# A path that is not taken: its transfers move from SyncE to GpSimd, and ScalarE issues the store of its last output tile

## The chip, the cores and the metric

One core of one Trainium2 chip runs the kernel. The metric is device time in microseconds: three runs of the kernel gave 161.3, 161.39 and 161.57, median 161.39. A further execution was taken with the hardware profiler; its own time was 161.53.

## The reference

Four batches with eight heads of 768 tokens and 64 channels each. An 8 x 8 matrix per head, made doubly stochastic in five rounds, mixes the eight blocks of 96 keys and values; attention runs inside each block; a gated MLP follows, whose gate mixes tokens with a 768 x 768 matrix.

```
for _ in range(5):
    P = exp(P - max(P)); P /= sum(P, rows) + 1e-9; P /= sum(P, columns) + 1e-9
k_sorted, v_sorted = P @ blocks of k, P @ blocks of v
attn = softmax(scale * q_b @ k_sorted.T) @ v_sorted          # inside blocks of 96
h = relu(x @ w_in); u, v = halves of h                       # x: heads side by side
v_n = (v - mean(v)) / sqrt(var(v) + 1e-6)
out = (u * (w_spatial @ v_n + b_spatial)) @ w_out
```

## The kernel before

The kernel has two versions of the whole computation. The *main path* is quick and leaves out the subtraction of maxima. It is written out by hand: the string `ORDER` (lines 18 to 51) lists some 300 short units by name and arguments, and the loop at line 769 records them one after the other. Every engine works through its own instructions in that order and waits on semaphores for the others. The *general path* (`general_path`, line 724) computes the same with maxima subtracted, in plain loops over batches and head pairs, using the same units.

Which of them gives the output is decided on the chip. Unit `CK` (line 694) compares row sums, column sums and reciprocals of the main path with bounds, `CF` (line 709) counts the violations into a flag, and `LF` (line 715) loads that flag into a register of each of the five engines. At line 773 each engine tests its register: with a flag above zero it runs the general path, otherwise it jumps over it. With the inputs drawn here the flag is zero and no instruction of the general path is executed. Unit `BH` (line 718) gives PE and VectorE a hint of the jump.

```
with tc.If(st["beyond"] > 0, preferred_fallthrough_block=True, label="general"):
    general_path()
```

For an If, the framework builds a second block, the *else block*, for the engines that jump. [...] So each engine that does something in the general path has in the else block, for each semaphore it would have raised, an instruction that waits until its main-path work is counted and then adds what the general path would have added. Transfers issued by SyncE or ScalarE count on eight semaphores in turn (the hardware transfers), those issued by GpSimd on eight others; for the latter one instruction of GpSimd, INC_SWDGE_SEM, adds to all eight. Then comes the *end block* (line 800 in the profile): SyncE waits for every semaphore once more in twelve steps, and after its drain all engines meet in a barrier which GpSimd gathers and releases, twice.

The output is stored by rows of 128 tokens. For the last batch (3), the six row blocks go one by one: `OH` multiplies, `OI` evicts PSUM to SBUF on ScalarE (`A`) or VectorE (`D`), `OJ` (line 690) issues the store, all on SyncE's queue. The last units of `ORDER` evict and store in this order:

```
... OI:D:3:0:0:512 OI:D:3:5:256:512 OI:A:3:4:0:512 OJ:3:1:0:512 OJ:3:5:256:512 OJ:3:4:0:512
OJ:3:0:0:512
```

Evictions are at lines 110 (ScalarE) and 112 (VectorE), the last stores at line 692, those of the batches before at line 645. In the general path SyncE loads `sort_net` (line 184), copies the block-shaped values (`VC`, line 418), transposes the attention output by DMA (`XD`, line 501) and stores the output (`OS`, line 645). `XT` (line 506) is a unit that makes the same transposition on TensorE, with a copy out of PSUM; the main path uses both.

Of the kernel before, what the change touches and what calls it, by code (L numbers as in the profile page):

```python
# [45 lines left out]
SH:3:3:0:0 GH:D:3:0:0 SH:0:3:0:1 OS:2:2 SH:1:3:1:1 GH:P:3:1:1 SH:2:3:3:1 OH:3:3:2:0:512:0:4 GH:D:3:0:1 OS:2:0:0:1  # L46
OS:2:0:1:2 OH:1:3:3:0:512:0:4 GH:P:3:3:1 OI:A:3:2:0:512 OI:A:3:3:0:512 OJ:3:2:0:512 OH:2:3:5:0:256:0:4 OJ:3:3:0:512
OH:0:3:5:256:512:0:4 OI:D:3:5:0:256 OH:3:3:1:0:512:0:4 OH:2:3:0:0:512:0:4 OI:A:3:1:0:512 OJ:3:5:0:256
OH:1:3:4:0:512:0:4 OI:D:3:0:0:512 OI:D:3:5:256:512 OI:A:3:4:0:512 OJ:3:1:0:512 OJ:3:5:256:512 OJ:3:4:0:512
OJ:3:0:0:512  # L50
"""

# [13 lines left out]
def kernel(  # L66
# [12 lines left out]
    nc = tc.nc  # L79

    B, H, S, D = q.shape
# [8 lines left out]
    KC = DM // 128  # L90
    FC = DH // 128
    HP = H // 2
# [11 lines left out]

    def ps_tile(n, dt=FP32):
        return psum.tile([128, 2, 512 if dt == FP32 else 1024], dt, name=f"ps{n}", tag=f"ps{n}")

    def copy(eng, out, in_):
        if eng == "A":
            nc.scalar.copy(out=out, in_=in_)  # L110
        else:
            nc.vector.tensor_copy(out=out, in_=in_)
# [9 lines left out]
    p_all = const.tile([BH, NB, NB], FP32, name="p_all")  # L122
# [27 lines left out]
    st = {}  # L150
# [30 lines left out]
            nc.gpsimd.dma_start(out=w_out_sb, in_=moe_w_out.rearrange("(fc p) n -> p fc n", p=128))  # L181

    def load_sort_net():
        nc.sync.dma_start(out=p_all, in_=sort_net.rearrange("b h i j -> (b h) i j"))

    def u_S0():
        load_sort_net()
# [37 lines left out]
    def u_SK(n, safe=False):  # L225
        n = int(n)
        rows, cols = (first[:, 0:NB], first[:, NB:2 * NB]) if n == 0 else (rowsum, colsum)
        over_rows = lambda x: x.to_broadcast([BH, NB, NB])
        over_cols = lambda x: _raw_ap(x, 0, [x.ap[0], [0, NB], x.ap[1]])
        if safe:  # L230
            nc.vector.reduce_max(out=rowsum, in_=p_all, axis=AX.X)
            nc.vector.tensor_sub(out=p_all, in0=p_all, in1=over_rows(rowsum))
        nc.scalar.activation(out=p_all, in_=p_all, func=AF.Exp)
        nc.vector.reduce_sum(out=rows, in_=p_all, axis=AX.X)
        if safe:
            nc.vector.tensor_scalar_add(out=rows, in0=rows, scalar1=1e-9)
        nc.vector.reciprocal(out=rowsum, in_=rows)
        nc.vector.tensor_mul(out=p_all, in0=p_all, in1=over_rows(rowsum))
        nc.vector.reduce_sum(out=cols, in_=p_all.rearrange("p i j -> p j i"), axis=AX.X)
        if safe:  # L240
            nc.vector.tensor_scalar_add(out=cols, in0=cols, scalar1=1e-9)
        nc.vector.reciprocal(out=colsum, in_=cols)
        to = p16.rearrange("p (i j) -> p i j", i=NB) if n == 4 else p_all
        nc.vector.tensor_mul(out=to, in0=p_all, in1=over_cols(colsum))
        if n == 4:
            nc.vector.transpose(out=p_t, in_=p16)

    def u_PR(ps):
        pr = ps_tile(ps)[:, 0, 0:NB * BH].rearrange("p (i y) -> p i y", i=NB)
        for i in range(NB):  # L250
            nc.tensor.matmul(
                pr[:, i, :], lhsT=spread[:, (i % NI) * NB:(i % NI + 1) * NB].rearrange("p j t -> p (j t)"),
                rhs=p_t[:, (i // NI) * BH:(i // NI + 1) * BH], start=True, stop=True,
            )
        st["pr"] = pr
# [6 lines left out]
    def u_P0(lo, hi):  # L262
        lo, hi = int(lo), int(hi)
        n, pr = hi - lo, st["pr"]
        nc.vector.tensor_mul(
            out=pd(0)[:, lo:hi].rearrange("p h (i t) -> p h i t", t=TB),
            in0=_raw_ap(mask16, 0, [mask16.ap[0], [0, n], [0, NB], [1, TB]]),
            in1=_raw_ap(pr, lo, [pr.ap[0], [1, n], [BH, NB], [0, TB]]),
        )

    def u_PC(eng):
        copy(eng, prep_sb, st["pr"])

    def u_PD(b, lo, hi):
        b, lo, hi = int(b), int(lo), int(hi)
        n = hi - lo
        nc.gpsimd.tensor_mul(
            out=pd(b)[:, lo:hi].rearrange("p h (i t) -> p h i t", t=TB),
            in0=_raw_ap(mask16, 0, [mask16.ap[0], [0, n], [0, NB], [1, TB]]),
            in1=_raw_ap(prep_sb, b * H + lo, [prep_sb.ap[0], [1, n], [BH, NB], [0, TB]]),  # L280
        )
# [103 lines left out]
    def u_KT(ps, eng, b, hp):  # L385
        mixed("k", "kT", ps, eng, int(b), int(hp))
# [14 lines left out]
    def u_VM(ps, eng, b, hp):  # L401
        b, hp = int(b), int(hp)
        t = ps_tile(ps)
        for hh in range(2):
            nc.tensor.matmul(
                t[:, hh, 0:G * D], lhsT=pd(b)[:, 2 * hp + hh, :], rhs=st["v", b][:, 2 * hp + hh, :],
                start=True, stop=True,
            )
        copy(
            eng,  # L410
            vm[:, :, 2 * hp:2 * hp + 2, 0:D].rearrange("p g h d -> p h g d"),
            t[:, :, 0:G * D].rearrange("p h (g d) -> p h g d", g=G),
        )

    def u_VC(b, lo, hi):
        b = int(b)
        for i in range(int(lo), int(hi)):
            nc.sync.dma_start(
                out=vb[b % 2][:, i].rearrange("c h d -> c (h d)"),
                in_=vm[i * TB:(i + 1) * TB].rearrange("t g h d -> t g (h d)"),  # L420
            )
# [75 lines left out]
    def u_XD(b, ih, lo=0, hi=4):  # L497
        b, ih, lo, hi = int(b), int(ih), int(lo), int(hi)
        if ("xT", b) not in st:
            st["xT", b] = att.tile([128, 2, KC, HW], BF16, name="xT", tag="xT", bufs=2)  # L500
        nc.sync.dma_start_transpose(
            out=st["xT", b][:, ih, lo:hi].rearrange("p k (i c) -> p (k i) c", i=NI),
            in_=st["x", b, ih][:, lo:hi].rearrange("p k i c -> p (k i c)"),
        )

    def u_XT(ps, eng, b, ih, lo):
        b, ih, lo = int(b), int(ih), int(lo)
        if ("xT", b) not in st:
            st["xT", b] = att.tile([128, 2, KC, HW], BF16, name="xT", tag="xT", bufs=2)
        t = ps_tile(ps, BF16)[:, 0, 0:2 * HW].rearrange("p (k i c) -> p k i c", k=2, i=NI)  # L510
        for k in range(2):
            for i in range(NI):
                nc.tensor.transpose(t[:, k, i, :], st["x", b, ih][:, lo + k, i, :], ident[0:BLK, 0:BLK])
        copy(eng, st["xT", b][:, ih, lo:lo + 2].rearrange("p k (i c) -> p k i c", i=NI), t)
# [54 lines left out]
    def u_LN(b, lo, hi):  # L569
        b, lo, hi = int(b), int(lo), int(hi)  # L570
        mv, rs = st["mv", b], st["rs", b]
        nc.scalar.activation(out=rs[:, lo:hi], in_=mv[:, lo:hi, 1], func=AF.Ln, bias=eps_tile[:], scale=1.0)
        nc.scalar.activation(out=rs[:, lo:hi], in_=rs[:, lo:hi], func=AF.Exp, bias=0.0, scale=-0.5)
# [66 lines left out]
            st["o", b, n0] = ld.tile([128, 3, DM], FP32, name="o_sb", tag="ld")[:, 0:2]  # L640
        copy(eng, st["o", b, n0][:, lo:hi], st["o_ps", b, n0][:, lo:hi])

    def u_OS(b, n0, lo=0, hi=2):
        b, n0, lo, hi = int(b), int(n0), int(lo), int(hi)
        nc.sync.dma_start(
            out=out[b].rearrange("(c p) n -> p c n", p=128)[:, n0 + lo:n0 + hi, :],
            in_=st["o", b, n0][:, lo:hi],
        )
# [38 lines left out]
        st["o1", b, n, c0] = ld.tile([128, 3, DM], FP32, name="o1_sb", tag="ld")[:, 0, 0:c1 - c0]  # L687
        copy(eng, st["o1", b, n, c0], st["o1_ps", b, n, c0])

    def u_OJ(b, n, c0, c1):  # L690
        b, n, c0, c1 = (int(x) for x in (b, n, c0, c1))
        nc.sync.dma_start(out=out[b, n * 128:(n + 1) * 128, c0:c1], in_=st["o1", b, n, c0])

    def u_CK():
        nc.vector.memset(bad, 0.0)
# [28 lines left out]
    def general_path():  # L724


        st.clear()
        load_sort_net()
        for n in range(5):
            u_SK(n, safe=True)  # L730
        u_PR(0)
        u_P0(0, 8)
        u_PC("A")
        for b in range(B):
            if b > 0:
                u_PD(b, 0, 8)
            for x in ("q", "k", "v"):
                u_L(x, b, 0, H)
            for hp in range(HP):
                u_VM(2, "A", b, hp)  # L740
            u_VC(b, 0, NB)
            for hp in range(HP):
                u_QN(2, "A", b, hp)
                u_KT(3, "D", b, hp)
                for ih in range(2):
                    u_SM(b, hp, ih)
                    u_AT(2, b, hp, ih)
            for ih in range(2):
                u_XD(b, ih, 0, HP)
            for n in range(0, G, 2):  # L750
                u_VP(n % 4, "A", b, n, n + 1)
                u_ST(b, n)
                u_ST(b, n + 1)
            u_LN(b, 0, G)
            for n in range(G):
                u_LA(b, n)
            for m in range(2):
                for ih in range(2):
                    u_UP(2 * m + ih, "A", b, m, ih)
            for mc in range(FC):  # L760
                u_SP(mc, b, mc)
                u_GT("D", b, mc)
            for n in range(0, G, 2):
                u_OP(n % 4, b, n)
                u_OE("A", b, n)
                u_OS(b, n)
# [38 lines left out]
```

## Time and profile before

| what | value |
|---|---|
| median of three runs | 161.39 us |
| the profiled execution's own time | 161.53 us |
| its span, first to last instruction | 159.7 us |
| granted TensorE clock, mean over the span | 0.996 |
| busy: PE / VectorE / ScalarE / GpSimd | 147.6 / 113.1 / 85.7 / 42.2 us |
| output stores on SyncE, 256 KB each | 7, median 2.6 us from issue to landing |

Busy time counts arithmetic alone; branches, semaphore steps and the issuing of transfers are not in it, and rows of an engine's sequencer carry a q after its name (SPq, ACTq). PE is busy through nearly all of the span except its very end, the last two of forty slices:

```profile
PE   6997989999999999999999999999999999899840
DMA  3999999999999999950000657300911377037253
```

The span ends with the last step of the barrier, not with the last store or the last piece of arithmetic. The profiled execution's own time is 1.8 us longer than its span.

### The profile page before, as it was taken

To read this page: it belongs to the slowest core of one execution; us is meant where nothing else is said; L and a number is where in the kernel's file an instruction comes from. 1 tells how busy PE (TensorE), PEld (TensorE's weight loads), DVE (VectorE), ACT (ScalarE), POOL (GpSimd) and SP (SyncE) were. 2 spreads that over 40 slices of the span, in tenths; PEclk is the share of its full clock that TensorE was granted. 3 is DMA by queue.
4 is the path that set the end of the run, shared out by engine and by line. 5 is a ranking of instruction groups with operands and counts; after the bars stand their busy time and mean duration, and the time that the engine had idled before them with its cause. 6 is when DMAs were issued, how large, how long until landed. Compare 5 with 4: busy or idle time off the path is not lost. (4 is left out here: it accounts for less than half of the span.)

```text
span 159.7 us, 3977 instructions
## 1 busy us (share of the span) xinstructions
PE 147.6 (92%) x1647; PEld 89.2 (56%) x1661; DVE 113.1 (71%) x261; ACT 85.7 (54%) x117; POOL 42.2 (26%) x46
## 2 busy tenths in 40 slices
PE   6997989999999999999999999999999999899840
PEld 2355867845686668556465654655655554455410
DVE  4786889638995679867838669897558956947620
ACT  3556799968889409478572446555432242340220
POOL 7942782292000034040000650210004440005300
PEclk9999999999999999999999999999999999999998
DMA  3999999999999999950000657300911377037253
GB/s 84 259 204 204 204 208 202 208 224 239 269 207 202 204 226 241 214 92 4 0 4 0 123 90 131 61 4 0 290 71 34 69 259 266 0 137 259 96 202 112
DMA packets 27526, 23.58 MB, mean 148 GB/s; under 512 B 7280, under 2 KB 24432, under 8 KB 27504
## 3 DMA queue, kind: packets, MB, share of 16 engines
q0 software_dynamic: 14352, 11.80, 46.6%
q1 hardware_dynamic: 13152, 11.49, 25.1%
q8 instruction: 14, 0.23, 0.6%
q14 instruction: 8, 0.07, 0.2%
HBM read 24.78 MB, written 6.29 MB: 195 GB/s over the span
## 5 line engine op out<-in xcount | busy, mean ns | idle before, releaser
L620 POOL TENSOR_TENSOR gt<-z,u_sb 128x768 bf16<-128x768 f32 x10 | 16.4, 1642 | 76.1 <-DVE rec_all L490 55.1
L442 ACT ACTIVATE ex<-ps 96x768 bf16<-96x768 f32 x32 | 24.4, 804 | 7.9 <-PE ps L437 7.8
L604 PE MATMUL ps<-wspT,v_sb 128*128 128x384 bf16 x144 | 25.4, 326 | 0.0
L592 PE MATMUL ps<-xT,w_in_sb 128*128 128x384 bf16 x128 | 23.3, 326 | 0.6 <-ACT o_sb L110 0.6
L491 DVE TENSOR_TENSOR x_sb<-ps,rec_all 96x512 bf16<-96x512 f32 x32 | 22.0, 687 | 1.1
L549 PE MATMUL ps<-w_in_sb,xT 128*128 128x512 bf16 x88 | 21.6, 379 | 0.5 <-issue 0.2
L566 DVE BATCH_NORM_STATS2 stats<-v_sb 128x6 f32<-128x512 bf16 x24 | 16.3, 680 | 5.5 <-ACT v_sb L116 4.3
L610 DVE TENSOR_TENSOR z<-ps,b_bc 128x768 f32<-128x768 f32 x12 | 11.5, 956 | 11.2 <-PE ps L604 11.2
L604 PEld LDWEIGHTS <-v_sb 128*128 128x128 bf16 x144 | 13.3, 98 | 8.4
L116 ACT ACTIVATE u_sb<-ps 128x768 bf16<-128x768 f32 x15 | 12.2, 812 | 10.8 <-PE ps L592 7.9
L116 ACT ACTIVATE v_sb<-ps 128x1024 bf16<-128x1024 f32 (+1 forms) x10 | 9.8, 982 | 14.4 <-PE ps L549 14.4
L592 PEld LDWEIGHTS <-w_in_sb 128*128 128x128 bf16 x128 | 11.8, 98 | 8.7 <-issue 0.9
L630 PE MATMUL ps<-w_out_sb,gt 128*128 128x512 bf16 x68 | 16.3, 379 | 0.2
L110 ACT COPY o_sb<-ps 128x1024 f32<-128x1024 f32 (+1 forms) x10 | 8.4, 839 | 14.7 <-PE ps L680 10.6
L549 PEld LDWEIGHTS <-xT 128*128 128x128 bf16 x96 | 8.9, 98 | 9.8
L483 PEld LDWEIGHTS <-ex 96*128 96x128 bf16 x256 | 10.9, 97 | 3.8 <-DVE x_sb L491 0.3
L483 PE MATMUL ps<-vb,ex 96*128 96x65 bf16 x256 | 12.4, 193 | 0.1
L110 ACT CAST kt<-ps 128x768 bf16<-128x768 f32 x12 | 9.3, 804 | 5.9 <-PE ps L378 5.9
L221 PE MATMUL ps<-warm 128*128 128x512 bf16 x35 | 10.0, 441 | 1.3 <-DVE warm L194 1.3
L630 PEld LDWEIGHTS <-gt 128*128 128x128 bf16 x72 | 6.6, 98 | 7.1
L437 PE MATMUL ps<-qT,kt 64*128 64x96 bf16 x256 | 9.3, 204 | 0.5 <-DVE x_sb L491 0.2
L490 DVE RECIPROCAL rec_all<-ps 96x8 f32<-96x8 f32 x32 | 6.3, 197 | 4.8 <-PE ps L483 4.4
(94 smaller groups left out, 198.5 us busy)
## 6 DMA issues: line engine op xcount, KB each, us to landing
out_dram<-o_sb SPq DMA_DIRECT2D x8, 512.0 KB, 3.7
k_in<-in_k_dram POOLq DMA_DIRECT2D x4, 768.0 KB, 23.9
v_in<-in_v_dram POOLq DMA_DIRECT2D x4, 768.0 KB, 22.8
vb<-vm SPq DMA_DIRECT2D x24, 99.0 KB, 5.6
q_in<-in_q_dram POOLq DMA_DIRECT2D x3, 768.0 KB, 29.0
out_dram<-o_sb SPq DMA_DIRECT2D x7, 256.0 KB, 2.6
ws_in<-in_moe_w_spatial_dram POOLq DMA_DIRECT2D x2, 576.0 KB, 27.8
w_in_sb<-in_moe_w_in_dram POOLq DMA_DIRECT2D x2, 512.0 KB, 23.9
```

The costliest lines, as they stand in the source:

```text
L110: nc.scalar.copy(out=out, in_=in_)
L116: nc.scalar.activation(out=out, in_=in_, func=AF.Relu)
L442: nc.scalar.activation(out=e_tile(b, hp, ih).rearrange("p h (x g) -> p h x g", g=G), in_=t[0:BLK, :, 0:HW].rearrange("p h (g x) -> p h x g ...
L483: nc.tensor.matmul(t[:, hh, ii * VW:ii * VW + D + 1], lhsT=e[:, c:c + 128], rhs=vb[b % 2][:, ih * NI + ii, 2 * hp + hh, 0:D + 1], start=Tr ...
L491: nc.vector.tensor_mul(out=x_sb[:, hp].rearrange("p i (h d) -> p h i d", h=2), in0=tv[:, :, :, 0:D], in1=_raw_ap(rec, 0, [rec.ap[0], [NI, ...
L549: nc.tensor.matmul(t[:, x, :], lhsT=st["xT", b][:, n // 3, kc, (n % 3) * 128:(n % 3 + 1) * 128], rhs=w_in_sb[:, kc, DH:DFF], start=(kc == ...
L566: nc.vector.bn_stats(out=stats, in_=st["v_sb", b, n])
L592: nc.tensor.matmul(t[:, x, 0:HW], lhsT=w_in_sb[:, kc, mc * 128:(mc + 1) * 128], rhs=st["xT", b][:, ih, kc, :], start=(kc == 0), stop=(kc = ...
L604: nc.tensor.matmul(t[:, x, 0:HW], lhsT=st["v_sb", b, n][:, mc * 128:(mc + 1) * 128], rhs=wspT[:, 3 * x:3 * x + 3, n, :], start=(n == 0), s ...
L610: nc.vector.tensor_add(out=z.rearrange("p (x c) -> p x c", x=2), in0=t[:, :, 0:HW], in1=b_bc.rearrange("p (x c) -> p x c", x=2),)
L620: eng.tensor_mul(out=gt, in0=st["z", b, mc], in1=st["u", b, mc // 2][:, mc % 2])
L630: nc.tensor.matmul(t[:, x, :], lhsT=st["gt", b, mc][:, (n0 + x) * 128:(n0 + x + 1) * 128], rhs=w_out_sb[:, mc, :], start=(mc == 0), stop=( ...
```

## The change

Two edits. In the general path every transfer that SyncE issued is issued by GpSimd, and the attention output is turned on TensorE by `XT` instead of by a DMA transpose, so that SyncE has nothing to do in that path. In the main path the last eviction of ScalarE, tile (3,4), is stored by a transfer that ScalarE issues itself; all others stay with SyncE.

```
-... OJ:3:1:0:512 OJ:3:5:256:512 OJ:3:4:0:512
+... OJ:3:1:0:512 OJ:3:5:256:512 OJ:3:4:0:512:A
 OJ:3:0:0:512

+    def queue(eng):
+        if "general" in st:
+            return nc.gpsimd
+        return nc.scalar if eng == "A" else nc.sync

     def load_sort_net():
-        nc.sync.dma_start(out=p_all, ...)
+        queue("S").dma_start(out=p_all, ...)
     def u_VC(b, lo, hi):
-            nc.sync.dma_start(
+            queue("S").dma_start(
-    def u_OS(b, n0, lo=0, hi=2):
+    def u_OS(b, n0, lo=0, hi=2, eng="S"):
-        nc.sync.dma_start(
+        queue(eng).dma_start(
-    def u_OJ(b, n, c0, c1):
+    def u_OJ(b, n, c0, c1, eng="S"):
-        nc.sync.dma_start(out=out[b, n * 128:(n + 1) * 128, c0:c1], in_=st["o1", b, n, c0])
+        queue(eng).dma_start(out=out[b, n * 128:(n + 1) * 128, c0:c1], in_=st["o1", b, n, c0])

     def general_path():
         st.clear()
+        st["general"] = True
 ...
             for ih in range(2):
-                u_XD(b, ih, 0, HP)
+                for lo in range(0, KC, 2):
+                    u_XT(2 + lo // 2, "A", b, ih, lo)
```

`queue` is new and needs no more than what is shown. Line numbers in the profile of the kernel after the change are a few higher: the stores of line 692 stand at 697, the If of line 773 at 780, the end block of line 800 at 807.

More of the change, by code (lines that the diff above doesn't have):

```diff
@@ L48 @@
 OH:0:3:5:256:512:0:4 OI:D:3:5:0:256 OH:3:3:1:0:512:0:4 OH:2:3:0:0:512:0:4 OI:A:3:1:0:512 OJ:3:5:0:256
-OH:1:3:4:0:512:0:4 OI:D:3:0:0:512 OI:D:3:5:256:512 OI:A:3:4:0:512 OJ:3:1:0:512 OJ:3:5:256:512 OJ:3:4:0:512
+OH:1:3:4:0:512:0:4 OI:D:3:0:0:512 OI:D:3:5:256:512 OI:A:3:4:0:512 OJ:3:1:0:512 OJ:3:5:256:512 OJ:3:4:0:512:A
 OJ:3:0:0:512
@@ L183, in load_sort_net @@
     def load_sort_net():
-        nc.sync.dma_start(out=p_all, in_=sort_net.rearrange("b h i j -> (b h) i j"))
+        queue("S").dma_start(out=p_all, in_=sort_net.rearrange("b h i j -> (b h) i j"))
     def u_S0():
```

## The prediction

> **What bounds the kernel now.** I read the page first, then the chain in order of time, then, because the chain stops long before the span does, the stretches, the transfers and the lines of the tail. The page's first line gives the span; the three lines after it are from the chain; the last two are stretches of the span (PE, PEld, DVE, ACT and POOL busy time with instruction counts, granted clock, DMA share, GB/s).
>
> ```profile
> span 159.7 us, 3977 instructions
> ...
> 150.36 3.32 PE ps L680 x17
> ...
> 153.75 0.59 ACT o_sb L110
> ...
> 154.40:158.00 3.60, 0.00 (x0) 0.00 (x0) 0.00 (x0) 0.00 (x0) 0.00 (x0) 1.00 0.54 194
> 158.00:159.70 1.70, 0.00 (x0) 0.00 (x0) 0.00 (x0) 0.00 (x0) 0.00 (x0) 0.65 0.00 0
> ```
>
> The last arithmetic is ScalarE's eviction of tile (3,4), over at 153.75 + 0.59 = 154.34. The other 5.4 us of the span hold no arithmetic: first the last stores, then 1.7 us in which not even a transfer runs. The change touches nothing that runs ahead of 154.34 (the main path keeps its order on every engine; I compared the two built programs), so only these 5.4 us can move. I therefore looked at VectorE's last evictions, at SyncE's last three issues one by one, and at the time from issue to landing of the last two.
>
> ```profile
> 152.84 1.02 DVE L112 COPY o_sb<-ps 128x512 f32<-128x512 f32 x2 [1.74 <-PE ps L680]
> 153.89 0.34 SPq L692 DMA_DIRECT2D out_dram<-o_sb  x1
> 154.36 0.62 SPq L692 DMA_DIRECT2D out_dram<-o_sb  x1
> 155.43 0.33 SPq L692 DMA_DIRECT2D out_dram<-o_sb  x1
> DMA to landing us min/median/max: 2.5/2.6/2.6
> ```
>
> The middle one is ScalarE's tile, issued 0.02 us after the eviction; the last one, VectorE's tile (3,0), stands behind it and leaves 1.07 us later, so the last byte lands near 155.43 + 2.5 = 157.9. Now the line of the If, where the general path is skipped.
>
> ```profile
> L773 SPq EVENT_SEMAPHORE  x8: 17/17/17, 156.0 to 158.0; - x8
> L773 POOLq EVENT_SEMAPHORE  x5: 17/42/43, 150.3 to 150.7; - x5
> L773 POOLq COMPARE_BRANCH  x1: 45/45/45, 149.1 to 149.1; - x1
> L773 POOLq INC_SWDGE_SEM  x1: 508/508/508, 150.8 to 150.8; - x1
> L773 DVEq COMPARE_BRANCH  x1: 84/84/84, 153.0 to 153.0; - x1
> L773 ACTq COMPARE_BRANCH  x1: 50/50/50, 153.8 to 153.8; - x1
> L773 DVEq EVENT_SEMAPHORE  x1: 21/21/21, 153.9 to 153.9; - x1
> L773 SPq COMPARE_BRANCH  x1: 58/58/58, 155.8 to 155.8; - x1
> L773 ACTq EVENT_SEMAPHORE  x1: 17/17/17, 156.6 to 156.6; - x1
> ```
>
> An engine that skips the path runs a small else block, which waits for its own work and adds to each semaphore what the skipped work would have added. SyncE's has one step for each of the eight semaphores of the hardware transfers; the last two of them wait for the last two landings, at 157.0 and 158.0 (first row). ScalarE branches at 153.8, but its one step runs at 156.6, though its eviction was over at 154.3. Then the end block:
>
> ```profile
> L800 SPq EVENT_SEMAPHORE  x12: 28/28/28, 158.0 to 158.7; - x12
> L800 SPq DRAIN  x2: 7/10/13, 158.8 to 158.8; - x2
> L800 POOLq EVENT_SEMAPHORE  x4: 17/17/17, 158.9 to 159.6; - x4
> L800 POOLq DRAIN  x3: 34/107/1461, 151.3 to 159.4; - x3
> L800 ACTq DRAIN  x2: 8/8/8, 156.7 to 159.1; - x2
> ```
>
> SyncE checks every semaphore again, twelve steps after the last landing; its drain releases GpSimd's gather at 158.9, and 0.8 us of barrier follow. So the end is the last landing + 0.9 + 0.8; ScalarE, at the barrier from 156.7 on, has about 2.1 us to spare.
>
> **The change part by part.** Counts are of the two built programs. In the general path SyncE goes from 103 instructions to 1, GpSimd from 32 to 94, ScalarE from 147 to 162, PE from 3420 to 3676, VectorE from 368 to 365; none is executed here. What is executed differs in three things.
>
> *SyncE's else block loses its eight steps.* Its queue is empty of them after its last issue, so it enters the end block while the stores still fly and runs ahead to the step of the first transfer that has not landed. Twelve steps take 0.7/11 = 0.064 us each, 0.76 us; the ten that need nothing late are hidden under a flight of 2.5 us, and about two remain after the last landing, 0.13. That takes some 0.6 us out.
>
> *The store of (3,4) goes to ScalarE.* SyncE drops that issue and the wait for it, and the one instruction queued behind, the store of (3,0), moves up: its data were ready by 152.84 + 1.02 = 153.86, so it leaves in the place of the removed one, at 154.3 to 154.4, and lands after 2.6 us, near 157.0. ScalarE's own issue starts at 154.37 and would, alone, also land near 157.0. Together they share the 16 DMA engines. In the stretch 154.40 to 158.00 the share is 0.54 of 3.60 us, 1.94 us for at most the 640 KB of the last three stores (256, 256 and 128), so 256 KB cost up to 0.78 us: the later one lands between 157.0 (no collision) and 157.8 (fully one behind the other). I take 157.3, nearer to the rows: until now the two flights overlapped too, and each still landed within 2.6.
>
> That 2.6 row stands for sharing as the trace has it. [...]
>
> *ScalarE is late to its branch.* No ScalarE issue is in this trace; the nearest rows are SyncE's, 0.33 to 0.62 us. Behind it on ScalarE's queue stand the branch (0.05), its else step and its drain, and SyncE's last step waits for ScalarE's semaphore too. So the branch is over at 154.37 + 0.33 + 0.05 = 154.75, up to 155.04. Then comes the wait seen today: from 153.8 + 0.05 to 156.6, 2.75 us. VectorE has one row pair of the same kind: branch at 153.0, step at 153.9, which is when its own eviction ended. I read ScalarE's 2.75 us as the fetching of the code it jumps to; VectorE and PE get a hint for it near the program's start, ScalarE does not:
>
> ```profile
> L800 DVEq BRANCH_PREFETCH_HINT  x1: 51/51/51, 0.8 to 0.8; - x1
> L800 PEldq BRANCH_PREFETCH_HINT  x1: 50/50/50, 0.8 to 0.8; - x1
> ...
> q1 hardware_dynamic: 565, 0.90, 39.6%
> q14 instruction: 4, 0.03, 2.0%
> ```
>
> The last two rows are the DMA queues in the window 153.5 to 159.7: four instruction packets move there beside the stores. The jump stays unhinted and a little longer (162 instructions instead of 147), so I keep 2.75. ScalarE's step then falls at 157.5 to 157.8, I take 157.6: later than the 157.3 of the landings. ScalarE becomes what SyncE waits for last.
>
> *GpSimd* takes 62 more instructions that it jumps over, and its one INC_SWDGE_SEM adds for 57 skipped transfers instead of 12. Today it is through at 151.3 + 1.46 = 152.8. Should its jump now cost ScalarE's 2.75 us, its else block starts at 151.9 instead of 150.3 and it ends at 154.4: hidden, with 3.2 us over until 157.6. *PE and VectorE* end at 154 and have as much cover. The transposes on TensorE are in the skipped path and cost nothing.
>
> Sum: ScalarE's step 157.6, SyncE's last step, drains and the gather 0.2 (158.7 to 158.9), barrier 0.8: span 158.6 instead of 159.7, 1.1 us less (1.2 to 0.9 by ScalarE's bounds, 0.8 if the landings are at 157.8). The profiled execution took 161.53 us, 1.8 around its span, which I leave as it is: 160.43. That execution lies 0.14 above the median of 161.39; on the median's scale the forecast is 160.3.
>
> **The rivals.** *ScalarE does not wait for code* after its jump, and the landings set the end: 157.2 + 0.13 + 0.2 + 0.8 = 158.3, 1.4 us less, 160.0. For it: nothing in the trace names the wait. Against: 156.6 stands in the row with no other work of ScalarE's to wait for. [...]
>
> *Within 0.2%* (0.32 us, about what a measurement of this kernel can tell from no change): ScalarE's first transfer costs it as much as the dearest output issue of SyncE,
>
> ```profile
> L645 SPq DMA_DIRECT2D out_dram<-o_sb x10: 373/538/1242, 112.6 to 143.3; - x10
> ```
>
> 1.24 us. Its step then comes at 154.37 + 1.24 + 0.05 + 2.75 = 158.4 and the end at 159.4: 0.3 less, 161.1. This is also the case that the store is not worth moving while the rest is.
>
> *Slower:* the six instructions left to ScalarE (two in the else block, four in the end block) fall across two pieces of code, and it fetches twice in turn: 154.8 + 2 x 2.75 = 160.3, + 0.2 + 0.8 = 161.3, 1.6 us more, 163.0. It decides as soon as ScalarE's waits after the jump pass 3.8 us (157.6 + 1.1 = 158.7 at its step). For it: the target moves by 16 instructions and the trace does not show where a piece ends. Against: six out of many; today one wait does.
>
> *Slower, on GpSimd:* its 2.0 us from 150.8 to 152.8 grow with the 57 transfers instead of 12, to 9.4, so it reaches the gather at 160.2 and the end is 161.0: 1.3 more, 162.7. It sets the end above 7.0 us (157.8) and makes the kernel slower above 8.1 (158.9). Against: still one instruction on eight semaphores.
>
> **How the numbers follow.** Forecast 0.64; no wait for code 0.15; within 0.2%, at 161.1, 0.11; two fetches 0.06; GpSimd 0.04. Faster by over 0.2%: 0.64 + 0.15 = 0.79; same 0.11; slower 0.10. The forecast's bounds reach from 160.2 to 160.6; the rival of 160.0, 0.2 lower where nothing collides, sets the low end at 159.8; the case of 161.1 sets the high end at 161.2; the two slower ones, 0.10, are left out.
>
> **What would show it.** In the profile after: no EVENT_SEMAPHORE of SyncE at the line of the If; about ten of its twelve end steps before 156; six issues of SyncE at the store's line, the last near 154.4, and one of ScalarE near 154.4; ScalarE's step at the If near 157.6 and SyncE's drain right behind. Wrong: ScalarE's step under 157.2 (first rival) or beyond 158.7 (slower), its issue over 1 us, a landing after 157.8, GpSimd's drain after 157.9, or any difference ahead of 154.3.

## The result, and the profile after

| | before | after |
|---|---|---|
| median, 8 runs each | 161.38 us | 160.96 us |
| lowest to highest | 161.26 to 161.57 | 160.58 to 161.11 |
| the profiled execution: time, span | 161.53, 159.7 | 160.97, 159.2 |

The ratio is 0.9969, with a 95% interval of 0.9958 to 0.998: the kernel is faster by 0.4 us. The forecast was 1.1 us, to 160.3. The measured time lies inside the range given, 159.8 to 161.2, but most of the forecast gain did not come.

The last arithmetic starts at 153.55 instead of 153.75. I take that as variation ahead of the change: in the traces below whose work up to there is the same, VectorE's step at the If, right behind its own last eviction, comes anywhere from 153.6 to 154.0 (153.9 in before, 153.7 after). I therefore count the *tail*, from the start of ScalarE's last eviction to the end of the span. It was 159.7 - 153.75 = 5.95 us and is 159.2 - 153.55 = 5.65. In the timeline after, the eviction, SyncE's last two issues (in one row) and ScalarE's issue:

```profile
153.55 0.59 ACT L115 COPY o_sb<-ps 128x512 f32<-128x512 f32 x1 [1.18 <-PE ps L685]
153.69 1.05 SPq L697 DMA_DIRECT2D out_dram<-o_sb  x2
154.17 0.38 ACTq L697 DMA_DIRECT2D out_dram<-o_sb  x1
```

The issues are as forecast: ScalarE's starts 0.03 us after its eviction and takes 0.38, and the store of (3,0) has moved up, to leave beside it. The line of the If:

```profile
L780 ACTq COMPARE_BRANCH  x1: 54/54/54, 154.6 to 154.6; - x1
L780 SPq COMPARE_BRANCH  x1: 54/54/54, 154.8 to 154.8; - x1
L780 ACTq EVENT_SEMAPHORE  x1: 17/17/17, 158.2 to 158.2; - x1
```

The end block's line (shortest, median and longest in ns; first and last start in us):

```profile
L807 SPq EVENT_SEMAPHORE  x14: 17/28/422, 155.3 to 159.1; - x14
L807 POOLq DRAIN  x3: 34/107/1461, 151.1 to 158.9; - x3
L807 SPq DRAIN  x3: 7/7/13, 158.3 to 158.6; - x3
```

SyncE's eight else steps are gone; its end steps begin at 155.3, and the longest, 422 ns, is the one that waits for ScalarE: SyncE's drain stands at 158.3, right behind ScalarE's step at 158.2. ScalarE sets the end, as forecast, but its wait after the branch is 158.2 - 154.65 = 3.55 us instead of 2.75. And the last landing is late too; at the stores' line, from issue to landing:

```profile
DMA to landing us min/median/max: 2.0/2.1/3.7
```

The 3.7 is the store of (3,0), issued at 154.07. The two stretches below, the DMA queues between ScalarE's branch and the first instruction packet behind it, and the half microsecond after that, show what moved while ScalarE waited:

```profile
q1 hardware_dynamic: 256, 0.36, 52.7%
q10 hardware_dynamic: 144, 0.26, 36.4%
```

From 154.65 to 156.6 SyncE's stores (q1) and ScalarE's (q10) took 89% of the 16 DMA engines, and not one instruction packet moved. From 156.6 to 157.1 two did:

```profile
q14 instruction: 2, 0.02, 7.7%
q1 hardware_dynamic: 2, 0.00, 0.2%
```

The rows do not say which engine a packet is for, and ScalarE's step, at 158.2, comes about 1.5 us behind the start of both. In before, the stretch from 153.85, ScalarE's branch there, to 154.75 holds two instruction packets beside a much lighter load:

```profile
q1 hardware_dynamic: 67, 0.10, 32.0%
q14 instruction: 2, 0.02, 7.7%
```

These rows suggest theory A, which the experiments have to decide: ScalarE's code is fetched by the DMA engines that carry the stores, and by issuing a store before it branches ScalarE lets its code fetch fall behind the last 512 KB. Rivals: B, that a transfer issued by ScalarE lengthens the wait whatever it carries; C, that the longer jump does.

### The profile page after: what moved, and what is told of

It is laid out like the page before. It is cut to its first block, busy times and chain, and to the rows that moved or that the text cites. A ratio compares the mean times of both kernels' runs of the same rounds, so it can differ in the third digit from the quotient of the medians.

```text
span 159.2 us, 3982 instructions
## 1 busy us (share of the span) xinstructions
PE 148.7 (93%) x1661; PEld 89.2 (56%) x1661; DVE 113.1 (71%) x261; ACT 85.8 (54%) x117; POOL 42.2 (26%) x46
## 5 line engine op out<-in xcount | busy, mean ns | idle before, releaser
L554 PE MATMUL ps<-w_in_sb,xT 128*128 128x512 bf16 x96 | 22.6, 379 | 0.0
```

The costliest lines, as they stand in the source:

```text
L554: nc.tensor.matmul(t[:, x, :], lhsT=st["xT", b][:, n // 3, kc, (n % 3) * 128:(n % 3 + 1) * 128], rhs=w_in_sb[:, kc, DH:DFF], start=(kc == ...
```

## The experiments

Each ratio is to runs of the kernel before taken alongside. Besides the time, I give ScalarE's wait (end of its branch to its step at the If) and the tail, each from the one profiled execution and, as the rows give tenths of a microsecond, good to about 0.1 us.

### Half the change: the path alone

```
-... OJ:3:4:0:512:A
+... OJ:3:4:0:512
```

> The general path's transfers on GpSimd as in the kernel after, the store of (3,4) back on SyncE. Times as in the trace of before, last eviction at 153.75. Theory A (ScalarE's code fetch waits behind store packets: its branch, 0.8 us earlier here, gets its fetch in before the stores flow): ScalarE's step at the If again at 156.6, 2.75 after its branch; the third store again leaves SyncE at 155.4 and lands at 157.9; end 157.9 + 0.13 + 0.2 + 0.8 = 159.0, 0.6 to 0.7 us under before: 160.7, a little under the kernel after. Theory B (a transfer issued by ScalarE lengthens the wait after its branch, whatever the stores do): the same as A. Theory C (the longer jump, 162 instructions instead of 147, costs more): the step at 157.4, 3.6 after the branch, same end.

160.45 us, ratio 0.9938 (0.9923 to 0.9952): faster than the whole change, and 0.25 under what was expected. Tail 158.7 - 153.46 = 5.24 us. ScalarE at the If, then SyncE in the end block from 155.6 to 158:

```profile
L780 ACTq COMPARE_BRANCH  x1: 50/50/50, 153.5 to 153.5; - x1
L780 ACTq EVENT_SEMAPHORE  x1: 17/17/17, 156.1 to 156.1; - x1
```

```profile
L807 SPq EVENT_SEMAPHORE  x12: 28/28/28, 155.7 to 157.8; - x12
L807 SPq DRAIN  x2: 7/10/13, 157.8 to 157.9; - x2
```

The wait is 2.55 us, a little under before, with the same longer jump as after: C falls. SyncE's steps run in the flight of the stores, and its drain, at 157.8, follows its last step at once. The skipped path's move is worth 0.7 us of tail.

### The other half: the store alone

The kernel after with SyncE's transfers, and the DMA transposes, back in the general path (`general_path` no longer sets the marker that `queue` tests).

> The store of (3,4) issued by ScalarE, the general path as before (SyncE has its eight else steps). A and B: ScalarE's wait after the branch is 3.5 us, its step at 158.3 to 158.4 on before's scale, but SyncE's eight else steps and twelve end steps follow the last landing at about 158.0, so SyncE sets the end: 158.0 + 0.9 + 0.8 = 159.7, within 0.2 us of before: 161.2 to 161.4. C: ScalarE's wait back at 2.75, step at 157.5, same end.

161.18 us, ratio 0.9985 (0.9973 to 0.9997): about 0.2 us. The wait is 158.1 - 154.55 = 3.55, which C missed: this kernel has the shorter jump of before. A miss of all theories is who ends last: the last landing came at 157.2, SyncE's twelve steps were at their last one by 157.9, and that waited for ScalarE after all.

### ScalarE gets the hint

```
-    "general", hint="LikelyTaken", engines=[mybir.EngineType.PE, mybir.EngineType.DVE])
+    "general", hint="LikelyTaken", engines=[mybir.EngineType.PE, mybir.EngineType.DVE, mybir.EngineType.Activation])
```

> The kernel after, with ScalarE among the engines that get the hint of the jump. All theories that put ScalarE's wait down to fetching code (A, B, C): its step comes right after its branch, under 155.5, and the landings set the end. A adds that no fetch stands among the last store packets: last landing 157.0 to 157.3 on before's scale, end at 158.1 to 158.4, 1.3 us under before: 160.1. If the late packets of the last landing in the kernel after (157.8 against 156.9 for the others) have another cause, the landing stays near 158.0 and the end is 159.0: 160.7. If the wait is not for code, nothing changes against the kernel after: 160.96.

160.09 us, ratio 0.9911 (0.9896 to 0.9927), tail 158.2 - 153.54 = 4.66: the forecast's whole gain and 0.2 more, from one word. ScalarE at the If, then SyncE's last steps in the end block, from 157.2 on:

```profile
L780 ACTq COMPARE_BRANCH  x1: 68/68/68, 154.6 to 154.6; - x1
L780 ACTq EVENT_SEMAPHORE  x1: 17/17/17, 155.1 to 155.1; - x1
```

```profile
L807 SPq EVENT_SEMAPHORE  x1: 28/28/28, 157.3 to 157.3; - x1
L807 SPq DRAIN  x2: 7/10/13, 157.3 to 157.4; - x2
```

With the hint, a BRANCH_PREFETCH_HINT of 50 ns on ScalarE at 0.8 us, the wait falls to 0.4 us; I therefore read it as a wait for code. In before one instruction packet moves at 157.3, 0.7 us behind ScalarE's step at 156.6; so the place of the two packets in the kernel after does not by itself say what ScalarE waited for. SyncE's last step now passes at 157.3 and waits for nothing else: the landings are the bound.

### Less to store

In the kernel after, row blocks 0 and 4 are stored with 64 of their 512 columns; the others are not written.

```
+        w = 64 if n in (0, 4) else c1 - c0
-        queue(eng).dma_start(out=out[b, ..., c0:c1], in_=st["o1", b, n, c0])
+        queue(eng).dma_start(out=out[b, ..., c0:c0 + w], in_=st["o1", b, n, c0][:, 0:w])
```

> The kernel after with the last two stores cut to 64 of their 512 columns (the other output columns of row blocks 0 and 4 of batch 3 are not written). A: nothing stands before the code fetch, ScalarE's wait after its branch falls from 3.56 back to 2.75 us, its step at 157.4 on before's scale, the end at 158.4: 1.2 us under before, 160.2. B and C: the wait stays at 3.5 us, the step at 158.3 and the time at 160.9.

160.12 us, ratio 0.9919 (0.99 to 0.9938). ScalarE at the If:

```profile
L781 ACTq COMPARE_BRANCH  x1: 54/54/54, 154.5 to 154.5; - x1
L781 ACTq EVENT_SEMAPHORE  x1: 17/17/17, 157.3 to 157.3; - x1
```

157.3 - 154.55 = 2.75 us: with most of the bytes gone and ScalarE's issue still there, the wait is what it was before, although the other stores still kept the DMA engines 56% busy in the microsecond from 154.6 on. B falls.

Then one store at a time, `if n == 0` (SyncE's) and `if n == 4` (ScalarE's):

> The kernel after with SyncE's last store, (3,0), cut to 64 of 512 columns (the rest of row block 0 of batch 3 is not written); ScalarE's store is whole. A (code fetch behind store packets): half the bytes stand in the way, ScalarE's wait after its branch lies between the 2.74 us of both stores cut and the 3.56 of none, 2.9 to 3.3, time 160.3 to 160.6. If it is ScalarE's own store alone that delays it (theory B in its milder form, its own queue): it stays at 3.5, and 160.9.

> The same with ScalarE's store, (3,4), cut to 64 columns and SyncE's whole. A: again between, 2.9 to 3.3 us, 160.3 to 160.6. B in its milder form: 2.75, and 160.1.

160.43 us, ratio 0.9932 (0.9913 to 0.9951), and 160.46 us, ratio 0.9934 (0.9912 to 0.9956). The branches and steps, SyncE's store cut first:

```profile
L781 ACTq COMPARE_BRANCH  x1: 54/54/54, 154.5 to 154.5; - x1
L781 ACTq EVENT_SEMAPHORE  x1: 17/17/17, 157.6 to 157.6; - x1
```

```profile
L781 ACTq COMPARE_BRANCH  x1: 54/54/54, 154.6 to 154.6; - x1
L781 ACTq EVENT_SEMAPHORE  x1: 17/17/17, 157.6 to 157.6; - x1
```

3.0 us in both. The wait grew with the bytes, 2.75, 3.0 and 3.55 us with none, one and two whole stores issued just ahead of the branch, and it made no difference whose store it was. The instruction packets moved with it: the first one behind the branch starts 1.2, 1.4 and 2.0 us after it (155.7 with both stores cut, 155.9 and 156.0 with one, 156.65 in the kernel after). Together with the hint this is what A says, though no row ties a packet to ScalarE.

### A late branch without a store

The kernel before, with three idle copies behind ScalarE's last eviction.

> The kernel before, with three more copies of 128 x 512 on ScalarE behind its last eviction (into a tile that nobody reads), so that it branches about 0.8 us later, near where it does in the kernel after, without issuing a transfer. A (the code fetch waits behind store packets): its wait from the branch to its step at the If grows from 2.75 to 3.2 us or more. B (a transfer issued by ScalarE is what lengthens it): it stays at 2.75. SyncE sets the end in both, as in before: 161.3 to 161.6.

161.21 us in its one run, just under what was expected. The branch came at 155.45, 0.8 us later than aimed at, and the wait was 158.3 - 155.45 = 2.85: neither theory's number clearly. SyncE alone issued the stores. The DMA engines were not idle: from 155.49 to 156.7 stores took 85% of them, yet one instruction packet moved among them, at 156.0, and a second right behind them. So A's 3.2 us or more did not come: 0.38 MB moved in this stretch, about what moved behind the branch with one store cut, and yet the wait is 2.85 and not 3.0. This run leaves open why.

### The hint without ScalarE's store

> The general path on GpSimd, the store of (3,4) on SyncE, and ScalarE among the engines with the hint: the hint's kernel without ScalarE's store. If it is ScalarE's code fetch that holds SyncE's third issue back by 0.45 us, that issue leaves 0.4 us earlier, the last landing comes 0.4 earlier than with the store on SyncE and no hint, and the time is 160.1, as with ScalarE's store and the hint: the store's move is then worth nothing by itself. If the spacing of SyncE's issues has another cause, it stays at 160.4 to 160.5, and ScalarE's store is worth 0.3 to 0.4 us once the hint is there.

160.66 us, ratio 0.995 (0.9935 to 0.9966). ScalarE's step comes at 154.4, and SyncE's third issue still left late: the first theory here falls, the code fetch does not hold SyncE. Without ScalarE's store the hint brings nothing that can be told from the path alone (0.995 against 0.9938, with intervals that overlap); with the hint, ScalarE's store is worth 160.66 - 160.09 = 0.6 us, while without it the same store costs 160.96 - 160.45 = 0.5.

### Another order of SyncE's stores

`OJ:3:0:0:512` moved ahead of `OJ:3:5:256:512`, with the hint; the store of (3,4) once by ScalarE and once, last, by SyncE.

> The kernel after with ScalarE's hint and the stores of (3,0) and of the half tile (3,5) exchanged in SyncE's queue: (3,0) is evicted 0.3 us before the half tile and no longer waits behind it. With the landings as the bound it leaves 0.6 us earlier, ScalarE's store becomes the last to land, and the end comes 0.3 to 0.5 us before that of the hint alone: 159.6 to 159.8. If the 16 DMA engines are the bound from the first of the three stores on, the last landing moves by 0.1 at most: 160.0.

> The same exchange with the store of (3,4) on SyncE, behind the two others: it then leaves as SyncE's third, 0.4 to 0.5 us after ScalarE would have issued it. If issuing by ScalarE is worth something where no code fetch interferes, this is 0.2 to 0.4 us slower than the exchange with ScalarE's store: about 160.0; if not, the same.

160.2 us, ratio 0.9916 (0.9897 to 0.9934), and 160.62 us, ratio 0.995 (0.9931 to 0.997). The exchange changes neither kernel by more than the noise (the first one's runs lie between 159.66 and 160.43): the expected 0.3 to 0.5 us did not come, so the order in SyncE's queue is not the bound. That fits the rival that the 16 engines are the bound, which gave 160.0; the times alone do not show it. ScalarE's store is again worth 0.4 us once its branch is hinted.

### SyncE's list one instruction shorter

```
     def u_BI():
-        nc.sync.dma_start(
+        nc.scalar.dma_start(
```

on the path alone, without and with the hint. SyncE had been idle 0.45 us between its last two issues in several kernels; in the path alone the timeline has

```profile
154.10 0.53 SPq L697 DMA_DIRECT2D out_dram<-o_sb  x1
155.09 0.33 SPq L697 DMA_DIRECT2D out_dram<-o_sb  x1
```

> Path on GpSimd, store of (3,4) on SyncE, no hint, and the load of the bias (in the middle of the kernel) issued by ScalarE instead of SyncE: SyncE's list is one instruction shorter. In before, in the path alone and in the path with the hint, SyncE stood idle 0.45 us between its last two issues; in the kernel after the same 0.47 us stand behind its branch, two instructions earlier in its list. Theory P: the 0.45 us belong to a place in SyncE's code (80 instructions in), not to the stores. Then they move behind the last issue here, the third store leaves at 154.6 rather than 155.1, the last landing and the end come 0.4 us earlier: 160.0 to 160.1. Rival (the queue of stores, or code fetches of other engines, hold the issue back): the gap stays before the last issue and the time at 160.45.

> The same with ScalarE's hint. P: as without it, 160.0 to 160.1, since ScalarE's step at 156.1 was not what the end waited for; its fetch packet among the store packets goes away, worth 0.1 at most. Against the kernel after with the hint (160.09): no difference, so ScalarE's store is worth nothing once SyncE's gap is out of the way. Rival (ScalarE's store is worth 0.5 by itself): 160.5.

161.6 us, ratio 1.0004 (0.9993 to 1.0015), and 161.63 us, ratio 1.0002 (0.999 to 1.0014): no gain in time, but the gap moves as theory P says. Without the hint, the timeline of SyncE's last two issues, its branch at the If, and VectorE's longest wait between 40 and 65 us:

```profile
155.26 1.28 SPq L697 DMA_DIRECT2D out_dram<-o_sb  x2
```

```profile
L780 SPq COMPARE_BRANCH  x1: 58/58/58, 157.0 to 157.0; - x1
```

```profile
DVE z L615 <- DMA b_bc<-in_moe_b_spatial_dram: 4.0, 1, 4.0
```

The last two issues follow each other with hardly a gap, and the 0.45 us stand behind them, from 155.26 + 1.28 = 156.54 to the branch at 157.0. With the hint it is the same: the two issues are over at 155.39 + 1.24 = 156.63, the branch comes at 157.1. Without the hint the tail fell from 5.24 to 159.5 - 154.65 = 4.85 us. But ScalarE gets to the bias load 12 us later than SyncE did (48.0 instead of 35.6), VectorE waits 4.0 us for it, and the last eviction starts 1.2 us later. With the hint the tail is 159.8 - 154.69 = 5.1 us, no better, so the saving of 0.4 us rests on one profiled execution; the expected 160.0 was missed in both. That ScalarE's store is worth nothing once this gap is out of the way stays open: the two times carry the bias load's loss.

## Why the prediction was right or wrong

*SyncE's else block, 0.6 us: right.* The path alone shortens the tail by 5.95 - 5.24 = 0.7, and the end steps run where they were said to.

*ScalarE's issue and branch: right.* 0.38 us for the issue (0.33 to 0.62 was given), the branch over 154.65 - 153.55 = 1.1 us after the eviction's start (1.0 to 1.3).

*ScalarE's wait after the branch, 2.75 us: the step that failed.* It is 3.55. The prediction read the wait as code fetching, which the fall to 0.4 us with the hint bears out, quoted the four instruction packets that move beside the stores, and then kept a number measured when the branch came ahead of the stores, for a branch that it had itself put behind them. It weighed the sharing of the 16 engines for the stores and not for the code. The bounds went over the issue's cost alone, where the term with the larger uncertainty was the wait. These 0.8 us are the whole miss of the span: with them the forecast's sum gives 159.4 on before's scale, and 159.2, as measured, with the eviction 0.2 earlier. That the time still lies inside the range is luck: the high end stood at 161.2 for the case of a dear issue, which did not happen.

*The landings, 157.3, at most 157.8 on before's scale: too early, but not what set the end.* The eviction starts 0.2 earlier after the change, so the last step, which the landing of (3,0) held until 157.8, stands for 158.0. ScalarE's tile was in by the time it was needed; the store of (3,0) took 3.7 us and landed 4.25 us after the eviction's start. In the store alone and in the hint's kernel, with the same two stores, it landed 157.2 - 153.44 and 157.3 - 153.54, 3.8 us, after it, which is 157.5 on before's scale. One of these kernels has the long wait for code and one has not, so that wait alone does not make the landing late; the cause stays open. One reading under this term was off by little: the stretch of 1.94 us was put to at most 640 KB, but its 194 GB/s over 3.60 us are 0.70 MB, so 256 KB cost 0.73 us rather than 0.78. The upper bound, one store landing fully behind the other, was 157.8; the trace after has the landing near there. With the hint, 160.09 with ScalarE's store against 160.66 without it, moving the issue was worth 0.6 us; how much of that is SyncE's time for the issue, 0.62 us in before, and how much is the gap in SyncE's list, below, is not shown.

*Why SyncE's second-to-last and last issue stood 1.07 us apart* was read as queueing behind the removed store. Of the 1.07, 0.62 are the issue and 0.45 belong to a place in SyncE's code; the change takes two instructions from SyncE's list, and the 0.45 us then stand behind the branch, from 154.85 to the first end step at 155.3, in the flight of the stores.

*GpSimd: right.* Its longest drain is 1461 ns as before, with 57 skipped transfers instead of 12, and ends at 152.6. *Barrier: right*, 1.0 us from ScalarE's step to the end.

*The rivals.* "No wait for code" did not happen by itself, but its 160.0 is what the hint gives, 160.09: the price of the missing hint was worked out rightly (it took the landing at 157.2 where the sum had 157.3; with 157.3 it gives 160.1). Without the hint ScalarE waited 2.55 to 3.55 us behind its branch in every trace. "Within 0.2%", at 161.1, came near the time for a wrong reason: the lost 0.7 us were put on the issue, and they sit in the wait behind it. No slower case came.

## What to carry to other kernels

Before an engine that is off the critical path is given the last store, look at what it still has to do behind it: here a jump, after which ScalarE, branching right behind the last two stores, waited 3.55 us instead of 2.75, so that half the change was better than the whole (160.45 against 160.96). The wait measured ahead of the stores, 2.75 us, was no price for the same wait behind them. Where a path is skipped at the end of a kernel, give the hint to the engine whose wait sets the end, and keep engines that wait for the last landing out of the skipped path: together with ScalarE's store that took the kernel to 160.09, the lowest median of those run. Where ScalarE's wait did not set the end, in the path alone, the hint brought nothing (160.66 with it, 160.45 without).

## What the runs showed of the hardware

ScalarE's wait after its unhinted jump, which I read as a wait for code, was 2.55 to 2.75 us where it branched ahead of the last stores or these were cut short, 3.0 behind one store of 256 KB and 3.55 behind two; behind SyncE's stores alone, in the late branch, it was 2.85. With the hint it was 0.4 to 0.5. Not every unhinted jump was followed by such a wait: SyncE's first step in before came 0.2 us after the start of its branch. SyncE stood still for 0.45 us at one place of its instruction list: between its last two issues in before (154.98 to 155.43) and in the path alone, behind the last issue where the list was one instruction shorter (156.54 to 157.0), behind the branch where it was two shorter (154.85 to 155.3 in the kernel after); why is not shown. And a store landed late for no reason that I found: the same last store was through 4.25 us after the last eviction's start in the kernel after, and 3.8 in the store alone and with the hint, in one execution each.
